# Attention over two pairs of heads at a time: column sums in 32-column quarters of one bank, reciprocals spread by transfers, float32 scores

## The chip, the cores and the metric

The kernel runs on one core of one Trainium2 chip. The metric is the device time of one launch in microseconds (us), a median over runs. The engines are TensorE (PE, with its weight loads as PEld), VectorE (DVE), ScalarE (ACT), GpSimd (POOL) and SyncE (SP), which here only issues transfers.

## What is computed

Float32 throughout, with sizes B=2, H=12, S=448, D=64; 896 tokens of width 768.

```python
scores = cap * tanh(q @ k.T / 8 / cap)            # 24 heads, 448 x 448
attn = exp(scores - max) ; attn /= attn.sum(-1) + 1e-9
x = (attn @ v)                                    # -> 896 x 768
xn = x / sqrt(mean(x*x, -1) + 1e-6) * rms_g
x = (silu(xn @ w_gate) * (xn @ w_val)) @ w_out    # 768 -> 1536 -> 768
out = ((x @ w1) * (x @ w2)) @ w3 @ w_out2         # 768 -> 1024 -> 1024 -> 768
```

## The kernel before

Everything is kept transposed: features on the partitions, tokens on the free axis. The 24 heads form 12 pairs p (a head in rows 0 to 63, the other in rows 64 to 127), and pairs 2d and 2d+1 form a block d of seven groups g (42 groups in all). Keys are cut in chunks of 128, three for each head (c = 0, 1, 2), and 64 keys are left over per head (c = 3). `parts(g)` (L373) says what a group holds: three groups of the even pair, one with the leftovers of both pairs, three of the odd pair. A group passes four steps:

- `scores` (L418, matmul in L430): keys x queries into a double bank `pss` (tag "s", 2 of them), one half for each head. Pair 0 multiplies in float32. For the others `load_head` (L380) splits queries and keys in two fp32r parts (`th`: `half` on ACT or POOL, `rest` L189 on DVE), and three fp32r products are added up. For c < 3 two matmuls with 64 rows each stand in the two row halves of the array; for c = 3 one matmul has 128 rows (the unneeded half of the keys is zero).
- `tanh` (L438) and `exp` (L444) on ACT, into a tile `t` (4 of them).
- `pv` (L448, matmul in L464), once for each pair in the group: the values (64 columns) of both heads into the two column halves of a bank `po`, then 64 columns of ones likewise into a bank `pn`, which gives each column sum 64 times. All four are float32 matmuls; the profile shows each float32 matmul as two records. `po` and `pn` are the two buffers of tag "o", so one pair holds both.
- at a pair's end `take_sum` (L468) and `take` (L478) empty both banks (ACT or DVE), `invert` (L484) takes reciprocals in two pieces (DVE), `normalize` (L491, DVE or POOL) multiplies, `square` (L499, ACT) and `add_square` (L510) gather the squares for the later norm. `normalize_x` (L343) finishes the norm of a batch: `sums` (L305), a root, reciprocals, six products, six splits.

Beside this the first half of the last product, w3 x w_out2, is made from weights alone (`last_product` L609, matmuls L634 to L636): 16 items of four steps of three fp32r matmuls each, into banks of tag "m" (2 of them). It fills PE where nothing else is ready, and most of it comes behind the attention. It reads the tile "B", which the normed x of batch 1 takes over. `weights` (L241) brings every weight tile: a load on SP, two unary operations (ACT or POOL), `join` L270 and `sign` L274 (DVE), a `half` (ACT or POOL) and a `rest` (DVE). `experts` (L719) does the rest of the network in fp32r, its banks taken in turn from tags "m", "o", "s".

The order on every engine is fixed before the launch: `Plan` (L53) holds tasks with a rank, a cost guess for each engine that may do it, and the buffers it makes or uses, and lists them by a simulated clock (`order` L87). Buffers of a tag are handed out in order of the rank of the task that makes them. Each engine then works its list strictly in order.

Of the kernel before, what the change touches and what calls it, by code (L numbers as in the profile page):

```python
# [33 lines left out]
CQ = S // 4  # L34

# [131 lines left out]
def body(ctx: ExitStack, tc, qk, v, cap, wgv, wdn, rg, w12, w3t, wo2, out):  # L167
# [44 lines left out]
    def layer(es, bounded):  # L212
# [5 lines left out]
        rings = dict(qk=2, th=3, v=3, t=4, sm=2, sq=2, s=2, o=2, m=2, raw=NRAW, hl=NHL, mo=2, sg=4, acc=2)  # L218
# [81 lines left out]
        def x_steps(b):  # L300
            st = {}

            def sums(e):
                st["pq"] = bank("o")
                e.matmul(st["pq"][:, :S], ones, acc[b], start=True, stop=True)  # L305
# [37 lines left out]
        def normalize_x(b, after, rank):  # L343
            sums, root, inverse, mul, first, second = x_steps(b)
            pq = buf("o")
# [12 lines left out]
        def attend():  # L358
# [7 lines left out]
            raws, heads, vals, chunks, pos, sums, sqs = {}, {}, {}, {}, {}, {}, {}  # L366
            qkb, thb = {p: buf("qk") for p in range(1, NP)}, {p: buf("th") for p in range(NP)}
            vb, tb, ob = {p: buf("v") for p in range(NP)}, {g: buf("t") for g in range(NG)}, {i: buf("o") for i in range(BH)}
            smb, sqb = {p: buf("sm") for p in range(NP)}, {p: buf("sq") for p in range(NP)}
            first_of = lambda p: 7 * (p // 2) + 3 * (p % 2)  # L370
            h_done, v_done = {}, {}

            def parts(g):  # L373

                d, r = divmod(g, 7)
                if r == 3:
                    return [(2 * d, 3), (2 * d + 1, 3)]
                return [(2 * d + (r > 3), r if r < 3 else r - 4)]

            def load_head(p):  # L380
                def one(e):
                    heads[p] = [ring(ap, "th", [P, 2, S + KP], F32, "qk0")[:, 0]]
                    e.dma_start(out=heads[p][0][:, : S + P], in_=qk[p][:, : S + P])

                def two(e):
                    e.dma_start(out=heads[p][0][:, S + P :], in_=qk[p][:, S + P :])

                def whole(e):
                    raws[p] = ring(ap, "qk", [P, S + KP])
                    e.dma_start(out=raws[p], in_=qk[p])  # L390
# [9 lines left out]
                when = first_of(p) - 7  # L400
                if p == 0:
                    a = add(("SP", 0.45), one, when, makes=[thb[p]], size=P * (S + P) * 4)
                    b = add(("SP", 0.45), two, when + 0.1, behind=[a], uses=[thb[p]], size=P * (KP - P) * 4)
                    h_done[p] = [a, b]
                    return
                a = add(("SP", 0.45), whole, when, makes=[qkb[p]], size=P * (S + KP) * 4)
                r = first_of(p) - 3
                a = add(dict(ACT=1.0, POOL=1.3), first, r, after=[a], makes=[thb[p]], uses=[qkb[p]])
                h_done[p] = [add(("DVE", 1.2), second, r, after=[a], uses=[qkb[p], thb[p]])]
# [38 lines left out]
            def pv(g, j):  # L448

                use = parts(g)  # L450
                p, c = use[j % len(use)]

                def run(e):
                    start = p % 2 == 0 and c == 0 or p % 2 == 1 and c == 3
                    stop = p % 2 == 0 and c == 3 or p % 2 == 1 and c == 2
                    if start:
                        pos[p] = [ring(ps, "o", [P, 512], name=name) for name in ("po", "pn")]
# [10 lines left out]
            def take_sum(pr):  # L468
                def run(e):
                    sums[pr] = ring(ap, "sm", [P, S])  # L470
                    if e is nc.scalar:
                        e.activation(sums[pr], pos[pr][1][:, :S], AF.Identity, bias=guard)
                    else:
                        e.tensor_scalar(sums[pr], pos[pr][1][:, :S], guard, None, op0=ALU.add)  # L474

                return run

            def take(pr):  # L478
                def run(e):
                    half(x_tile(*divmod(pr, H // 2)), pos[pr][0][:, :S], e)  # L480

                return run

            def invert(pr, c):  # L484
                def run(e):
                    r = sums[pr][:, c * S // 2 : (c + 1) * S // 2]
                    e.reciprocal(r, r)  # L487

                return run

            def normalize(pr):  # L491
                def run(e):
                    b, h = divmod(pr, H // 2)
                    x = xraw[b][:, h, :]
                    e.tensor_tensor(x, x, sums[pr], op=ALU.mult)
# [3 lines left out]
            def square(pr):  # L499
                def run(e):  # L500
# [5 lines left out]
                    e.activation(sqs[pr] if h else acc[b], xraw[b][:, h, :], AF.Square)  # L506
# [13 lines left out]
            exps, x_alloc, sq_last, pv_last = {}, {}, {}, {}  # L520
            every = []
            for g in range(NG):
                use = parts(g)
                sb = buf("s")
                qs = [thb[p] for p, _ in use]
# [3 lines left out]
                us = 0.62 * 2 if len(use) == 2 else 0.72  # L529
                if use[0][0] == 0:  # L530
                    us = 0.83 + 0.62 if len(use) == 2 else 0.97
                a = add(("PE", us), scores(g), g - 2, after=need, makes=[sb], uses=qs)
                a = add(("ACT", 1.02), tanh(g), g, after=[a], makes=[tb[g]], uses=[sb])
                exps[g] = a = add(("ACT", 1.06), exp(g), g + 0.1, after=[a], uses=[tb[g]])
                for j in range(len(use)):
                    p, c = use[j]
                    begin = p % 2 == 0 and c == 0 or p % 2 == 1 and c == 3
                    end = p % 2 == 0 and c == 3 or p % 2 == 1 and c == 2
                    both = [ob[2 * p], ob[2 * p + 1]]
                    a = add(  # L540
                        ("PE", 1.65), pv(g, j), g + 1 + 0.1 * j, after=[exps[g], v_done[p], pv_last.get(p)],
                        makes=both if begin else [], uses=[tb[g], vb[p]] + ([] if begin else both),
                    )
# [12 lines left out]
                    every.append(a)  # L556
                    a = add(("ACT", 0.58), square(p), r + 0.4, after=[a], makes=[sqb[p]] if h else [], uses=[xb[b]])
# [51 lines left out]
        def last_product():  # L609
# [16 lines left out]

            def item(kb, n, r):
                def run(e):
                    if r == 0:
                        mb[kb, n] = bank("m")  # L630
# [10 lines left out]
            for kb in range(CF2):  # L641
                bb = [buf("m") for _ in range(2)]
# [13 lines left out]
        def attend_any():  # L656
# [4 lines left out]
            for i in range(BH):  # L661
# [5 lines left out]
                nc.sync.dma_start(out=tv, in_=v[pr])  # L667

# [50 lines left out]
        def experts(over, stored):  # L719
# [258 lines left out]
            for D in range(CD // 2):  # L978
# [72 lines left out]
                for n, (name, op, ready) in enumerate(jobs):  # L1051
# [13 lines left out]
                    tag = ("m", "o", "s")[turn // 2 % 3]  # L1065
# [94 lines left out]
```

## Time and profile before

| | us |
|---|---|
| median of 3 runs (641.0 to 644.27) | 641.41 |
| the profiled execution | 643.46 |
| its span, first to last instruction | 641.7 |
| PE busy | 623.0 (97%) |
| DVE busy | 421.2 (66%) |
| ACT busy | 279.7 (44%) |
| POOL busy | 154.3 (24%) |

The profile lists busy time by engine, then the chain of work that ended last, and groups of instructions by line; the views of the trace cut the same records by stretch, by line, or in order of time. A PE that is busy may be busy with work that another form would need less of; an engine's idle time counts only where PE, or the end, waits for it.

### The profile page before, as it was taken

To read this page: it belongs to the slowest core of one execution; us is meant where nothing else is said; L and a number is where in the kernel's file an instruction comes from. 1 tells how busy PE (TensorE), PEld (TensorE's weight loads), DVE (VectorE), ACT (ScalarE), POOL (GpSimd) and SP (SyncE) were. 2 spreads that over 40 slices of the span, in tenths; PEclk is the share of its full clock that TensorE was granted. 3 is DMA by queue.
4 is the path that set the end of the run, shared out by engine and by line. 5 is a ranking of instruction groups with operands and counts; after the bars stand their busy time and mean duration, and the time that the engine had idled before them with its cause. 6 is when DMAs were issued, how large, how long until landed. Compare 5 with 4: busy or idle time off the path is not lost.

```text
span 641.7 us, 8149 instructions
## 1 busy us (share of the span) xinstructions
PE 623.0 (97%) x3141; PEld 513.8 (80%) x3141; DVE 421.2 (66%) x532; ACT 279.7 (44%) x384; POOL 154.3 (24%) x148
## 2 busy tenths in 40 slices
PE   6989999998999999999999999999999999999995
PEld 2334445468999999999999999999999999999995
DVE  2999969568857778534666555566656765636752
ACT  6878889834634434222334323334423333313230
POOL 2755421002223354321122222211122121100000
PEclk9999999999999999999999999999999999999999
DMA  8445511125634445423994233333232324105111
GB/s 301 127 134 186 166 41 50 34 70 189 227 140 152 148 147 192 153 66 120 314 285 143 99 102 111 129 103 99 98 99 98 110 88 131 34 0 147 54 47 63
DMA packets 29759, 80.18 MB, mean 125 GB/s; under 512 B 2960, under 2 KB 18448, under 8 KB 29712
## 3 DMA queue, kind: packets, MB, share of 16 engines
q1 hardware_dynamic: 29712, 79.58, 37.4%
q8 instruction: 27, 0.44, 0.3%
q14 instruction: 20, 0.16, 0.1%
HBM read 70.52 MB, written 9.04 MB: 124 GB/s over the span
## 4 chain that ended last, share of the span: by engine, by line
PE 89%; DVE 3%; DMA 3%; ACT 2%; POOL 1%; SPq 0%; issue 0%; DVEq 0%; ACTq 0%; POOLq 0%
PE bank L803 22%; PE bank L801 22%; PE bank L802 22%; PE bank L1025 8%; PE po L464 5%; PE pn L464 4%; PE pss L430 4%; DMA wraw<-in_wgv 1%; PE bank L634 1%; DMA wraw<-in_wo 1%; PE bank L636 1%; PE bank L635 1%; DVE sm L487 1%; DVE wraw L274 1%; DVE wraw L270 0%
## 5 line engine op out<-in xcount | busy, mean ns | idle before, releaser
L189 DVE TENSOR_TENSOR whl<-wraw,whl 128x768 fp32r<-128x768 f32 (+1 forms) x86 | 75.9, 884 | 68.3 <-POOL whl L186 55.7
L266 POOL TENSOR_SCALAR wraw<-wraw 128x768 int32<-128x768 uint32 (+1 forms) x67 | 75.1, 1120 | 160.8 <-DMA wraw<-in_w 58.2
L802 PE MATMUL bank<-xn,whl 128*128 128x448 f32 x288 | 105.6, 367 | 0.0
L803 PE MATMUL bank<-xn,whl 128*128 128x448 f32 x288 | 105.6, 367 | 0.0
L801 PE MATMUL bank<-xn,whl 128*128 128x448 f32 x288 | 105.6, 367 | 0.0
L270 DVE SCALAR_TENSOR_TENSOR wraw<-wraw 128x768 int32<-128x768 int32 (+1 forms) x76 | 72.4, 952 | 40.8 <-POOL wraw L266 39.9
L274 DVE SCALAR_TENSOR_TENSOR wraw<-wraw 128x768 int32<-128x768 int32 (+1 forms) x76 | 74.4, 978 | 1.6
L186 POOL TENSOR_SCALAR whl<-wraw 128x768 fp32r<-128x768 f32 (+1 forms) x35 | 32.2, 919 | 171.4 <-PE bank L803 124.1
L182 ACT ACTIVATE whl<-wraw 128x768 fp32r<-128x768 f32 (+1 forms) x51 | 40.7, 800 | 70.9 <-PE bank L803 30.4
L801 PE MATMUL bank<-y,whl 128*128 128x448 f32 x192 | 70.7, 368 | 0.0
L802 PE MATMUL bank<-y,whl 128*128 128x448 f32 x192 | 70.7, 368 | 0.0
L803 PE MATMUL bank<-y,whl 128*128 128x448 f32 x192 | 70.7, 368 | 0.0
L257 ACT ACTIVATE wraw<-wraw 128x768 f32<-128x768 f32 (+1 forms) x57 | 49.8, 874 | 45.5 <-DMA wraw<-in_wgv 15.0
L801 PEld LDWEIGHTS bank<-xn,whl 128*128 128x128 f32 x288 | 54.1, 188 | 4.9
L803 PEld LDWEIGHTS bank<-xn,whl 128*128 128x128 f32 x288 | 54.1, 188 | 4.9
L802 PEld LDWEIGHTS bank<-xn,whl 128*128 128x128 f32 x288 | 54.1, 188 | 4.7
L802 PE MATMUL bank<-u,whl 128*128 128x448 f32 x144 | 52.8, 367 | 0.0
L803 PE MATMUL bank<-u,whl 128*128 128x448 f32 x144 | 52.8, 367 | 0.0
L801 PE MATMUL bank<-u,whl 128*128 128x448 f32 x144 | 52.8, 367 | 0.0
L464 PE MATMUL po<-t,v 128*64 128x448 f32 (+1 forms) x192 | 46.0, 557 | 3.4 <-DVE sm L474 1.8
L438 ACT ACTIVATE t<-pss,small 128x896 f32<-128x896 f32 x42 | 42.0, 999 | 11.9 <-PE pss L430 8.7
L444 ACT ACTIVATE t<-t,small 128x896 f32<-128x896 f32 x42 | 43.8, 1043 | 1.3
(105 smaller groups left out, 1013.5 us busy)
## 6 DMA issues: line engine op xcount, KB each, us to landing
wraw<-in_wgv SPq DMA_DIRECT2D x24, 768.0 KB, 4.6
wraw<-in_w SPq DMA_DIRECT2D x16, 768.0 KB, 4.3
wraw<-in_wdn SPq DMA_DIRECT2D x12, 768.0 KB, 4.3
wraw<-in_w3t SPq DMA_DIRECT2D x16, 512.0 KB, 3.5
wraw<-in_wo SPq DMA_DIRECT2D x8, 768.0 KB, 6.5
qk<-in_qk SPq DMA_DIRECT2D x11, 480.0 KB, 3.7
m_half<-mo SPq DMA_DIRECT2D x16, 192.0 KB, 2.5
mo<-m_half SPq DMA_DIRECT2D x16, 192.0 KB, 5.0
```

The costliest lines, as they stand in the source:

```text
L189: e.tensor_tensor(lo, raw, r32(hi), op=ALU.subtract)
L257: e.activation(h, h, AF.Copy, scale=2.0**-112)
L266: e.tensor_scalar(l, l.bitcast(U32), 0.876 * 2.0**-29, 0.49, op0=ALU.mult, op1=ALU.add)
L270: e.scalar_tensor_tensor(l, h, 3, l, op0=ALU.logical_shift_left, op1=ALU.bitwise_or)
L274: e.scalar_tensor_tensor(l, h, -(2**31), l, op0=ALU.bitwise_and, op1=ALU.bitwise_or)
L438: e.activation(chunks[g], s[:, :, :S], AF.Tanh, scale=tsc)
L444: e.activation(chunks[g], chunks[g], AF.Exp, scale=acap)
L464: e.matmul(pos[p][n][to, :S], w, x, start=start, stop=stop)
L801: e.matmul(dst, whi[:, c, :], src(0, g, b), start=(g == 0), stop=False)
L802: e.matmul(dst, whi[:, c, :], src(1, g, b), start=False, stop=False)
L803: e.matmul(dst, wlo[:, c, :], src(0, g, b), start=False, stop=(g == total - 1))
L1025: e.matmul(st["bank", name], w[:, q, :], z_at(op, q, y), start=q == 0 and n == 0, stop=q == NQ - 1 and n == 2)
```

## The change

Scores are one float32 product for every pair; the splits of queries and keys go. A block's groups alternate between its two pairs, and the leftovers of both come last (r = 6), in four 64 x 64 quarters of the array. `pv` makes values only. The column sums of a block's four heads come from `total`: four matmuls with 32 columns of ones each, which fill the four quarters of one bank (tag "os"), once for each chunk. Sums are emptied and inverted once for each block; `spread` then copies each head's 32 rows of reciprocals to the 64 rows where `normalize` wants them, by four transfers for each pair. Sums are emptied and products taken on DVE only, squares go from ACT to DVE or POOL. "m" has one bank, and the items of the last product behind the fourth take turns between "o", "m" and "s". The layout of the leftover values is swapped for odd pairs.

```diff
-        rings = dict(qk=2, th=3, v=3, t=4, sm=2, sq=2, s=2, o=2, m=2, raw=NRAW, hl=NHL, mo=2, sg=4, acc=2)
+        rings = dict(qk=4, v=4, t=7, sm=2, rb=3, sq=3, s=2, o=2, os=1, m=1, raw=NRAW, hl=NHL, mo=2, sg=4, acc=2)
...
-                st["pq"] = bank("o")
+                st["pq"] = bank("os")
...
+            first_of = lambda p: 7 * (p // 2) + p % 2
...
-                if r == 3:
+                if r == 6:
                     return [(2 * d, 3), (2 * d + 1, 3)]
-                return [(2 * d + (r > 3), r if r < 3 else r - 4)]
+                return [(2 * d + r % 2, r // 2)]
+
+            def across(p, i):
+
+                return slice(D, P) if (p + i) % 2 else slice(0, D)
 
             def load_head(p):
-                def first(e):
-                    t = ring(ap, "th", [P, 2, S + KP], F32R)
-                    heads[p] = [t[:, 0], t[:, 1]]
-                    half(t[:, 0], raws[p], e)
-
-                def second(e):
-                    rest(heads[p][1], raws[p], heads[p][0], e)
-
...
+                when = first_of(p) - (7 if p == 0 else 5)
+                cuts = [slice(0, S + P), slice(S + P, S + KP)] if p == 0 else [slice(0, S + KP)]
...
-                    for n, (x, y) in enumerate(((0, 0), (0, 1), (1, 0))):
-                        for j in range(2):
-                            p, c = use[j % len(use)]
-                            if p == 0 and n:
-                                continue
-                            k, q = heads[p][x], heads[p][y]
-                            rows = slice(j * D, (j + 1) * D) if c < 3 else slice(0, P)
-                            ks = slice(S + c * P, S + (c + 1) * P)
-                            e.matmul(chunks[g][:, j, :S], k[rows, ks], q[rows, :S], start=n == 0, stop=p == 0 or n == 2)
+                    for j in range(2):
+                        for p, c in use:
+
+                            q = heads[p][j * D : (j + 1) * D]
+                            if c < 3:
+                                at, to, ks = j, slice(0, P), slice(S + c * P, S + (c + 1) * P)
+                            else:
+                                at, to, ks = p % 2, across(p, j), slice(S + 3 * P + j * D, S + 3 * P + (j + 1) * D)
+                            e.matmul(chunks[g][to, at, :S], q[:, ks], q[:, :S], start=True, stop=True)
 
                 return run
 
...
-                    for n in range(2):
-                        for i in range(2):
-                            to = slice(i * D, (i + 1) * D)
-                            rows = to if c == 3 else slice(0, P)
-                            x = chunks[g][rows, j if c == 3 else i, :]
-                            w = ones[rows, :D] if n else vals[p][rows, 6 if c == 3 else 2 * c + i, :]
-                            e.matmul(pos[p][n][to, :S], w, x, start=start, stop=stop)
-
...
+            def pv(g):
+
+
+                def run(e):
+                    for i in range(2):
+                        for p, c in parts(g):
+                            if c == 0 and i == 0:
+                                pos[p] = ring(ps, "o", [P, 512], name="po")
+                            rows, n = (slice(0, P), i) if c < 3 else (across(p, i), p % 2)
+                            w = vals[p][rows, 2 * c + i if c < 3 else 6, :]
+                            e.matmul(pos[p][i * D : (i + 1) * D, :S], w, chunks[g][rows, n, :], start=c == 0, stop=c == 3)
+
+                return run
+
+            def total(d, c):
+
+
+                def run(e):
+                    if c == 0:
+                        pns[d] = ring(ps, "os", [P, 512], name="pn")
+                    for q in range(4):
+                        p, i = 2 * d + q // 2, q % 2
+                        g, rows, n = (7 * d + 2 * c + q // 2, slice(0, P), i) if c < 3 else (7 * d + 6, across(p, i), p % 2)
+                        to = slice(q * CW, (q + 1) * CW)
+                        e.matmul(pns[d][to, :S], ones[rows, :CW], chunks[g][rows, n, :], start=c == 0, stop=c == 3)
+
+                return run
+
...
+            def spread(pr, i):
+
+
+                def run(e):
+                    if i == 0:
+                        rbs[pr] = ring(ap, "rb", [P, S])
+                    row = (2 * (pr % 2) + i // 2) * CW
+                    e.dma_start(out=rbs[pr][i * CW : (i + 1) * CW], in_=sums[pr // 2][row : row + CW])
...
-                    e.activation(sqs[pr] if h else acc[b], xraw[b][:, h, :], AF.Square)
+                    x = xraw[b][:, h, :]
+                    e.tensor_tensor(sqs[pr] if h else acc[b], x, x, op=ALU.mult)
...
+                c, last = use[0][1], use[-1][1] == 3
+                a = add(("PE", 0.83), pv(g), g + 1, after=[exps[g]] + [v_done[p] for p, _ in use] + [pv_last.get(p) for p, _ in use],
+                        makes=[ob[p] for p, c in use if c == 0], uses=[tb[g]] + [vb[p] for p, _ in use] + [ob[p] for p, c in use if c])
+                for p, _ in use:
                     pv_last[p] = a
-                    if not end:
-                        continue
-                    b, h = divmod(p, H // 2)
-                    r = g + 1.5
+                if use[-1][0] % 2 == 0:
+                    continue
+                d = g // 7
+                from_ = [g] if last else [g - 1, g]
+                t = add(("PE", 0.83), total(d, c), g + 1.2, after=[exps[x] for x in from_] + [sum_last.get(d)], makes=[] if c else [nb[d]],
+                        uses=[tb[x] for x in from_] + ([nb[d]] if c else []))
+                sum_last[d] = t
+                if not last:
+                    continue
+                r = g + 1.5
+                b = 2 * d // (H // 2)
+                taken = {}
+                got = add(("DVE", 0.64), take_sum(d), r - 2, after=[t], makes=[smb[d]], uses=[nb[d]])
+                for p in (2 * d, 2 * d + 1):
                     new = b not in x_alloc
-                    done = [add(dict(ACT=0.55, DVE=0.64), take_sum(p), r - 2, after=[a], makes=[smb[p]], uses=[both[1]])]
-                    done.append(add(dict(ACT=0.55, DVE=0.64), take(p), r - 1.9, after=[a] + ([] if new else [x_alloc[b]]),
-                                    makes=[xb[b]] if new else [], uses=[both[0]] + ([] if new else [xb[b]])))
-                    x_alloc.setdefault(b, done[1])
-                    inv = [add(("DVE", 1.52), invert(p, c), r + 0.1 * c, after=done, uses=[smb[p]]) for c in range(2)]
-                    a = add(dict(DVE=0.66) if h == 5 else dict(DVE=0.66, POOL=1.3), normalize(p), r + 0.3, after=inv, uses=[smb[p], xb[b]])
+                    taken[p] = add(dict(ACT=0.55, DVE=0.64), take(p), r - 2 + 0.1 * (p % 2), after=[a] + ([] if new else [x_alloc[b]]),
+                                   makes=[xb[b]] if new else [], uses=[ob[p]] + ([] if new else [xb[b]]))
+                    x_alloc.setdefault(b, taken[p])
+                inv = [add(("DVE", 1.52), invert(d, c), r + 0.1 * c, after=[got], uses=[smb[d]]) for c in range(2)]
+                for p in (2 * d, 2 * d + 1):
+                    h = p % (H // 2)
+                    sent = []
+                    for i in range(4):
+                        sent.append(add(("SP", 0.45), spread(p, i), r - 50, after=inv, behind=sent[-1:], makes=[] if i else [rbb[p]], uses=[smb[d]] + ([rbb[p]] if i else []), size=CW * S * 4))
+                    a = add(("DVE", 0.66), normalize(p), r + 0.3, after=sent + [taken[p]], uses=[rbb[p], xb[b]])
                     every.append(a)
-                    a = add(("ACT", 0.58), square(p), r + 0.4, after=[a], makes=[sqb[p]] if h else [], uses=[xb[b]])
+                    a = add(dict(DVE=0.66, POOL=1.3), square(p), r + 0.4, after=[a], makes=[sqb[p]] if h else [], uses=[xb[b]])
...
+            mtag = lambda kb, n: "m" if 2 * kb + n < MB else ("o", "m", "s")[(2 * kb + n - MB) % 3]
...
-                tag = ("m", "o", "s")[turn // 2 % 3]
+                tag = ("m", "o", "s", "os", "o", "s")[turn % 6]
```

## Rows read from the trace of the kernel before

**Rows 1.** The page's busy line of PE: us, share of the span, instructions.
```profile
PE 623.0 (97%) x3141; PEld 513.8 (80%) x3141; DVE 421.2 (66%) x532; ACT 279.7 (44%) x384; POOL 154.3 (24%) x148
```

**Rows 2.** Busy time by stretch: attention, the filler behind it, the experts, the end.
```profile
core 0: us, PE busy (x) PEld busy (x) DVE busy (x) ACT busy (x) POOL busy (x), PEclk, DMA share, GB/s
5.10:135.75 130.65, 126.52 (x677) 55.96 (x677) 105.05 (x109) 105.60 (x122) 50.57 (x44) 1.00 0.37 123
135.75:165.03 29.28, 26.59 (x151) 25.92 (x150) 22.52 (x25) 13.36 (x21) 5.39 (x7) 1.00 0.56 184
165.03:634.94 469.91, 469.87 (x2317) 431.88 (x2316) 292.06 (x391) 159.30 (x240) 97.93 (x92) 1.00 0.37 123
634.94:641.70 6.76, 0.00 (x0) 0.00 (x0) 0.62 (x1) 0.00 (x0) 0.00 (x0) 0.84 0.13 42
```

**Rows 3.** Waits of PE over the span: us in total, times, longest.
```profile
PE pss L430 <- DMA qk<-in_qk: 5.1, 1, 5.1
PE bank L634 <- ACT mo L182: 2.7, 1, 2.7
PE po L464 <- DVE sm L474: 1.8, 2, 1.3
PE po L464 <- DVE xraw L184: 1.5, 1, 1.5
PE pss L430 <- ACT t L438: 0.6, 2, 0.4
```

**Rows 4.** Busy time by stretch of L464 alone: PE, PEld, then clock and DMA.
```profile
5.10:135.75 130.65, 79.58 (x384) 24.22 (x384) 1.00 0.37 123
```

**Rows 5.** The chain of work, 44 to 64 us: start, us, what.
```profile
46.54 0.90 PE po L464 x4
47.44 0.75 PE pn L464 x4
...
49.70 0.80 PE pss L430 x6
```

**Rows 6.** PE in order of time around a leftover group: start, us.
```profile
39.06 0.97 PE L464 MATMUL po<-t,v 64*64 64x448 f32 x4
39.87 0.92 PE L464 MATMUL pn<-t,ones 64*64 64x448 f32 x4
40.72 0.87 PE L430 MATMUL pss<-th 64*128 64x448 f32 x6
```

**Rows 7.** Groups by line and form, 0 to 170 us: busy us, mean ns | idle before.
```profile
L444 ACT ACTIVATE t<-t,small 128x896 f32<-128x896 f32 x42 | 43.8, 1043 | 1.3
L438 ACT ACTIVATE t<-pss,small 128x896 f32<-128x896 f32 x42 | 42.0, 999 | 11.9 <-PE pss L430 8.7 <-PE pn L464 2.9
L487 DVE RECIPROCAL sm<-sm 128x224 f32<-128x224 f32 x24 | 35.6, 1522 | 1.0 <-ACT sm L472 0.8
L189 DVE TENSOR_TENSOR th<-qk,th 128x960 fp32r<-128x960 f32 x11 | 13.7, 1249 | 5.1 <-ACT th L182 5.1
L464 PEld LDWEIGHTS pn<-t,ones 128*64 128x64 f32 x144 | 10.3, 137 | 16.7 <-issue 16.7
L506 ACT ACTIVATE sq<-xraw 128x448 f32<-128x448 f32 x10 | 5.8, 576 | 7.5 <-POOL xraw L495 4.1 <-DVE xraw L495 3.2
L513 DVE TENSOR_TENSOR acc<-acc,sq 128x448 f32<-128x448 f32 x8 | 5.4, 676 | 1.4 <-ACT sq L506 1.4
```

**Rows 8.** Pair 0's three float32 score groups: by form, and the third in time.
```profile
L430 PE MATMUL pss<-qk 64*128 64x448 f32 x12 | 4.0, 820 | 5.1 <-DMA qk<-in_qk 5.1
...
8.16 0.93 PE L430 MATMUL pss<-qk 64*128 64x448 f32 x4
```

**Rows 9.** Loads at the start: one stretch (columns as rows 2), the page's issue line.
```profile
6.00:7.00 1.00, 1.00 (x6) 0.59 (x4) 0.00 (x0) 0.00 (x0) 0.00 (x0) 1.00 0.92 312
...
qk<-in_qk SPq DMA_DIRECT2D x11, 480.0 KB, 3.7
```

**Rows 10.** Tile mo to 170 us: the landing of its 192 KB transfers.
```profile
DMA to landing us min/median/max: 1.8/2.5/8.1
```

**Rows 11.** The chain of work behind the attention: start, us, what.
```profile
142.54 8.43 DMA wraw<-in_wgv
```

More of the change, by code (lines that the diff above doesn't have):

```diff
@@ L34 @@
 CQ = S // 4
+CW = P // 4
+MB = 4
 BOUND = 40.0
@@ L365, in attend @@
             NP = BH // 2
[L366 to L370, printed above, removed]
+            heads, vals, chunks, pos, pns, sums, rbs, sqs = {}, {}, {}, {}, {}, {}, {}, {}
+            qkb = {p: buf("qk") for p in range(NP)}
+            vb, tb, ob, nb = {p: buf("v") for p in range(NP)}, {g: buf("t") for g in range(NG)}, {p: buf("o") for p in range(NP)}, {d: buf("os") for d in range(NP // 2)}
+            smb, sqb = {d: buf("sm") for d in range(NP // 2)}, {p: buf("sq") for p in range(NP)}
+            rbb = {p: buf("rb") for p in range(NP)}
+            first_of = lambda p: 7 * (p // 2) + p % 2
             h_done, v_done = {}, {}
@@ L385, in two @@
[L385 to L390, printed above, removed]
-                def first(e):
-                    t = ring(ap, "th", [P, 2, S + KP], F32R)
-                    heads[p] = [t[:, 0], t[:, 1]]
-                    half(t[:, 0], raws[p], e)
-                def second(e):
-                    rest(heads[p][1], raws[p], heads[p][0], e)
@@ L400, in load_head @@
[L400 to L408, printed above, removed]
@@ L409, in load_head, with run @@
-                h_done[p] = [add(("DVE", 1.2), second, r, after=[a], uses=[qkb[p], thb[p]])]
+                def run(e, cols, new):
+                    if new:
+                        heads[p] = ring(ap, "qk", [P, S + KP])
+                    e.dma_start(out=heads[p][:, cols], in_=qk[p][:, cols])
+                when = first_of(p) - (7 if p == 0 else 5)
+                cuts = [slice(0, S + P), slice(S + P, S + KP)] if p == 0 else [slice(0, S + KP)]
+                h_done[p] = []
+                for n, c in enumerate(cuts):
+                    h_done[p].append(
+                        add(("SP", 0.45), lambda e, c=c, n=n: run(e, c, n == 0), when + 0.1 * n, behind=h_done[p], makes=[] if n else [qkb[p]], uses=[qkb[p]] if n else [],
+                            size=P * (c.stop - c.start) * 4)
+                    )
@@ L471, in run, with take_sum @@
+            def take_sum(d):
+                def run(e):
+                    sums[d] = ring(ap, "sm", [P, S])
                     if e is nc.scalar:
-                        e.activation(sums[pr], pos[pr][1][:, :S], AF.Identity, bias=guard)
+                        e.activation(sums[d], pns[d][:, :S], AF.Identity, bias=guard)
                     else:
-                        e.tensor_scalar(sums[pr], pos[pr][1][:, :S], guard, None, op0=ALU.add)
+                        e.tensor_scalar(sums[d], pns[d][:, :S], guard, None, op0=ALU.add)
@@ L479, in run, with invert @@
                 def run(e):
-                    half(x_tile(*divmod(pr, H // 2)), pos[pr][0][:, :S], e)
+                    half(x_tile(*divmod(pr, H // 2)), pos[pr][:, :S], e)
                 return run
-            def invert(pr, c):
+            def invert(d, c):
                 def run(e):
-                    r = sums[pr][:, c * S // 2 : (c + 1) * S // 2]
+                    r = sums[d][:, c * S // 2 : (c + 1) * S // 2]
                     e.reciprocal(r, r)
+                return run
[5 more added lines that the diff above has]
+                    e.dma_start(out=rbs[pr][i * CW : (i + 1) * CW], in_=sums[pr // 2][row : row + CW])
                 return run
@@ L494, in run @@
                     x = xraw[b][:, h, :]
-                    e.tensor_tensor(x, x, sums[pr], op=ALU.mult)
+                    e.tensor_tensor(x, x, rbs[pr], op=ALU.mult)
                 return run
@@ L519, in attend @@
                 load_val(p)
-            exps, x_alloc, sq_last, pv_last = {}, {}, {}, {}
+            exps, x_alloc, sq_last, pv_last, sum_last = {}, {}, {}, {}, {}
             every = []
@@ L524, in attend @@
                 sb = buf("s")
-                qs = [thb[p] for p, _ in use]
+                qs = [qkb[p] for p, _ in use]
                 need = []
@@ L528, in attend @@
                     need += h_done[p][:1] if p == 0 and c == 0 else h_done[p]
[L529 to L532, printed above, removed]
+                a = add(("PE", 0.83), scores(g), g - 2, after=need, makes=[sb], uses=qs)
                 a = add(("ACT", 1.02), tanh(g), g, after=[a], makes=[tb[g]], uses=[sb])
@@ L629, in run @@
                     if r == 0:
-                        mb[kb, n] = bank("m")
+                        mb[kb, n] = bank(mtag(kb, n))
                     whi, wlo = w3[kb]
@@ L641, in last_product @@
             for kb in range(CF2):
-                bb = [buf("m") for _ in range(2)]
+                bb = [buf(mtag(kb, n)) for n in range(2)]
                 last = {}
@@ L667, in attend_any @@
                 nc.sync.dma_start(out=tv, in_=v[pr])
+                if pr % 2:
+                    for j in range(2):
+                        nc.sync.dma_start(out=tv[j * D : (j + 1) * D, 6], in_=v[pr][(1 - j) * D : (2 - j) * D, 6])
                 off = one * (KP - S)
@@ L1125, in _layout @@
     v = a["v"].reshape(BH // 2, 2, S, D)
-    both = np.concatenate([v[:, 0, 3 * P :], v[:, 1, :D]], axis=1)[:, None]
+    both = np.stack([v[:, 0, 3 * P :], v[:, 1, :D]], axis=1)
+    both[1::2] = both[1::2, ::-1].copy()
+    both = both.reshape(-1, 1, P, D)
     v = np.stack([v[:, 0, : 3 * P].reshape(-1, 3, P, D), v[:, 1, D:].reshape(-1, 3, P, D)], axis=2).reshape(-1, 6, P, D)
```

25 lines of the change are left out of this document (2 added, 23 removed).

## The prediction

> **What bounds the kernel now.** I read the busy line first: PE is busy for 623.0 us of 641.7 [rows 1], so 18.7 us are idle, and any gain must come from less PE work or from that rest. Busy time by stretch comes next [rows 2]: the experts, 165.03 to 634.94, have PE busy for 469.87 of 469.91 us. The change leaves that stretch's products as they are, so its length stays and the question is only when it starts. The waits of PE [rows 3] place the idle time: 5.1 for the first load, 3.9 in the attention (1.8 and 1.5 for DVE emptying the banks of a pair, 0.6 for ACT), 2.7 behind it, and 6.76 at the end when the last output leaves [rows 2]. In the attention DVE is busy for 105.05 us and ACT for 105.60 of 130.65 [rows 2]: loaded, but PE seldom waits for either. So this is a PE sum, with DVE, ACT and transfers as possible new limits.
>
> **PE, values and sums.** Line 464 costs 79.58 us [rows 4] for 48 calls of `pv` (12 pairs, four chunks), 1.66 each: 0.90 for the values and 0.75 for the ones that follow [rows 5]. 0.75 is two float32 matmuls side by side in two column halves; the 0.15 above it falls on the first step after one of another tile shape. After the change there are 42 `pv` and 24 `total` (six blocks, four chunks), each a step of another shape than the one before it: 42 x 0.90 + 24 x 0.90 = 59.4. That is 20.2 less.
>
> The open price is that of four tiles at once, which no row shows. The lower bound is 0.75, as for two tiles [rows 5], or less than nothing extra where two steps of one shape meet (0.15 saved each). The upper bound is 1.50, two at a time, at each of 24 `total`, six leftover scores and six leftover `pv`. One reason for a small surplus: a 64-column weight load takes 137 ns [rows 7], and four of them in a row, 0.55, exceed the 0.375 of one of the two passes; that would make a `total` 1.10, 24 x 0.35 = 8.4 us more. But these loads run beside matmuls (24.22 us of them under 79.58 of matmuls [rows 4]) and 32 columns should need less. I take 0.75 plus the 0.15, nearest to the rows that show two tiles without any loss.
>
> The Trainium skill, TensorE: Matmul & The Clock Gate, section "Measured speedup vs the span model", has three column tiles at 2.38 times one, not 3. An estimate by it, a surplus of a quarter on each `total`, would add 24 x 0.19 = 4.6 us to my sum; no run here shows three or four tiles.
>
> **PE, scores.** A fp32r group costs 0.80 behind a `pv` [rows 5]. What is left of the stretch's 126.52 busy us, without the 79.58 of line 464 and some 10 of filler and norm (16 triples at 0.52, one 0.75, and shape changes), is 37 for 42 groups, 0.88 each (the leftover groups are dearer). A float32 group is two passes of two row halves: 0.75 + 0.15 = 0.90, 42 x 0.90 = 37.8, so 1 us more. Pair 0 speaks against it at first sight: its three float32 groups took 4.0 us, 1.33 each, with records of 820 ns [rows 8]. But that includes waiting, and the third, all four of its records, took 0.93 with its drain [rows 8], as a `po` step does in the same kind of view (0.97 [rows 6]). Were it 1.33 everywhere, 42 x 0.43 = 18 us would be added; a rival. PE in all: 20.2 - 1.0 = 19.2 less.
>
> **The start.** Group 1 now belongs to pair 1, so its scores wait for 480 KB more [rows 9], where before three groups of pair 0 ran on the first load. Behind the first 288 KB, which land at 5.1, stand 192, twice 224 and 480 KB, 1.15 MB; at 312 GB/s [rows 9] that is 3.7 us, 8.8 in all, and later if the weight loads behind share. Group 0 ends at about 6.5 (its records are slow [rows 8]), so PE loses about 2.5 us (bounds 0, if ACT sets the pace there anyway, to 5).
>
> **What leaves DVE, ACT and POOL.** The eleven splits of queries and keys take 13.7 us of DVE, half of 24 reciprocals 17.8 [rows 7]; squares come to DVE or POOL, at most 12 x 0.676 = 8.1 by the row of the nearest product [rows 7], and five products come from POOL to DVE, 3.4. DVE has about 20 us less, 85 for a stage of some 113. All this is off PE's path and worth only the waits of rows 3: 3.3 of the 3.9 are DVE's. I count 1.5 of them, since the new `po` banks are both in use and a block's end still waits for both to be emptied. ACT loses 12 squares (6.9) and about 4.5 of splits and sums. The splits that leave ACT and POOL free them for weight steps; I count nothing.
>
> **What is added off PE.** 48 spread transfers of 57 KB wait on SP for the reciprocals; queued behind them on SP are loads of later heads and weights, which are asked for five groups (some 11 us) ahead, so nothing is counted. Each `normalize` on DVE waits for its four transfers, with weight steps and the next squares queued behind it. The nearest row, 192 KB, lands in 1.8 to 8.1, median 2.5 [rows 10]; I take 2.5 with the issues before it, hidden under DVE's 28 us of slack. At the end of the attention the chain to the norm of batch 1 gains a spread and a second pair, perhaps 5 us; it is covered by the remaining items (at least nine of 2.1 us, 19) and by the four early products on batch 0. The cover before was 29.28 [rows 2]; if it fails, up to 5 us show. The stall of 2.7, a bank emptied late because ACT stood waiting for a load of 8.43 us [rows 3, 11], is kept (0 to 6).
>
> With one "m" bank an item waits for the emptying of the one before; attention work stands between, so nothing is counted, and moving items behind the attention moves PE work without adding any.
>
> **The sum.** Span: 641.70 - 19.2 + 2.5 - 1.5 = 623.5. The profiled execution adds 1.76 (643.46 - 641.70): 625.3. It is 2.05 above the median, so on the scale of the median **623.2 us**, 2.8% less.
>
> **Rivals.**
> 1. *ACT sets the pace of the attention.* Tanh and exp take 2.04 a group [rows 7]; the other ACT work of the stage, 105.6 - 85.8 - 11.4 = 8.4, adds 0.20. That is 2.24 against PE's 97.2 / 42 = 2.31, where before it stood at 2.51 against 2.78. For it: the margin shrinks from 0.27 to 0.07, and only two score banks stand between the engines. Against: `t` grows from 4 to 7 and items fill PE's gaps. Waits of 0.15 a group give 42 x 0.15 = 6: 629.5. Chance 0.18.
> 2. *DVE waits for the spreads.* DVE's slack of 28 us over 12 pairs is 2.3 each; it decides from a landing of 2.5 + 2.3 = 4.8 us behind the weight loads in the queues. At 6 us PE would lose 12 x 1.2 = 14: 637. For it: the 8.1 of rows 10. Against: half the landings are at 2.5 or less. Chance 0.10.
> 3. *Four tiles run two at a time,* slower than before: 36 steps x 0.75 = 27, 650. It decides from 0.5 us a step, where the gain is gone. For it: nothing shows four. Against: two halves of the array work with no loss in both directions, and four quarters are the same thing twice. Chance 0.08; float32 scores at 1.33 (641) have 0.02 more.
> 4. *Two row halves can't write one bank at once,* which the leftover scores and the leftover `total` do: 12 x 0.75 = 9, 632. The rows speak against it: in the leftover `pv` of before both row halves write one bank, and it takes 0.81 and 0.85 from start to start [rows 6], no more than the rest. The Trainium skill, TensorEngine Tiling (Array Packing), section "Gotcha 1: PSUM Pressure", says that different row tiles cannot access the same bank simultaneously; by that rule this rival holds, and the trace disagrees for halves of the partitions. Chance 0.02.
>
> That the change doesn't do what it says would be rival 3: sums of 32 columns that cost what 64 did.
>
> **How the numbers follow.** The forecast, PE's sum, has 0.60 and a range of its own of 614 to 630 (below: waits of 3.9 and 2.7 gone and shapes that meet, 9; above: weight loads not hidden and a late norm). A measurement of this kernel can tell about 0.5% from no change. Faster, under 638.2: 0.60 + 0.18 + 0.06 of rival 2 + 0.02 = 0.86. Slower, over 644.6: 0.08 + 0.02 = 0.10. Within: 0.04. The range that should hold 8 in 10 is 614 to 636; it takes in rival 1, rival 4 and the early part of rival 2.
>
> **What would show it.** In the profile after: line 464's values and the `total` steps at 0.75 to 0.90 from start to start, together near 59 us; L430 near 38; PE's busy time near 604; the first experts' product at about 147 instead of 165, and from there the same 470 us; a wait of PE for pair 1's load near 2.5. `total` near 1.65 would show rival 3; PE waiting for `t` over 42 groups rival 1; DVE idle ahead of `normalize` by more than 28 us in all rival 2. The prediction is wrong if the experts' stretch itself changes length, or if PE's idle time grows by more than 8 us.

## The result, and the profile after

The changed kernel takes 624.96 us (624.79 to 625.47) against 641.87 (641.0 to 644.27): a ratio of 0.9732, 95% interval 0.9704 to 0.976. The forecast was 623.2. The profiled execution took 625.47 with a span of 623.3; the sum had 625.3 and 623.5.

The page's busy line of the changed kernel, and what PE waited for (us in total, times, longest), as [rows 1] and [rows 3] of before:

```profile
PE 608.6 (98%) x3088; PEld 490.6 (79%) x3088; DVE 401.0 (64%) x527; ACT 265.7 (43%) x359; POOL 141.6 (23%) x138
...
PE pss L421 <- DMA qk<-in_qk: 5.1, 1, 5.1
PE po L449 <- ACT t L435: 2.2, 1, 2.2
PE bank L826 <- DVE whl L191: 0.8, 2, 0.6
PE bank L654 <- DVE mo L186: 0.4, 1, 0.4
PE bank L824 <- ACT mo L184: 0.3, 1, 0.3
```

PE's busy time fell by 14.4 us, not by 19.2, and its idle time fell from 18.7 to 14.7, where the sum had let it grow by 1.0. The waits for DVE in the attention are gone, all of them. Busy time by stretch (columns as [rows 2]: start, attention, hand-over to the experts):

```profile
5.10:15.00 9.90, 7.66 (x22) 2.39 (x24) 2.46 (x3) 4.26 (x5) 4.12 (x4) 1.00 1.02 401
15.00:114.50 99.50, 99.50 (x580) 26.56 (x580) 75.60 (x93) 86.83 (x93) 30.39 (x29) 1.00 0.42 135
114.50:160.00 45.50, 44.03 (x239) 41.36 (x236) 37.65 (x46) 21.08 (x34) 11.35 (x11) 1.00 0.60 192
```

From 15 us to the last sums at 114.5 PE is never idle; before, the attention ran to 135.75 [rows 2]. The chain of work of the changed kernel shows what a step costs from start to start (L449 values, L463 sums, L421 scores; the last two lines are leftovers of a block):

```profile
100.61 0.90 PE po L449 x4
101.52 0.89 PE pn L463 x8
102.41 0.95 PE pss L421 x4
106.83 0.91 PE pss L421 x8
...
113.68 0.93 PE pn L463 x8
```

Four tiles of 32 columns (0.89), and four quarters of 64 x 64 (0.91), cost what two tiles cost before (0.90 [rows 5]), each with its change of shape. The first products of the experts start at 145.68 instead of 165.03 (147 was said).

### The profile page after: what moved, and what is told of

Same layout as the page of the kernel before. It is cut to its first block, busy times and chain, and to the rows that moved or that the text cites. A ratio compares the mean times of both kernels' runs of the same rounds, so it can differ in the third digit from the quotient of the medians.

```text
span 623.3 us, 8065 instructions
## 1 busy us (share of the span) xinstructions
PE 608.6 (98%) x3088; PEld 490.6 (79%) x3088; DVE 401.0 (64%) x527; ACT 265.7 (43%) x359; POOL 141.6 (23%) x138
## 4 chain that ended last, share of the span: by engine, by line
PE 91%; DMA 3%; DVE 2%; ACT 2%; issue 1%; SPq 0%; DVEq 0%; ACTq 0%
PE bank L826 22%; PE bank L825 22%; PE bank L824 22%; PE bank L1048 8%; PE pss L421 6%; PE po L449 6%; PE pn L463 3%; DMA wraw<-in_wgv 2%; DMA m_half<-mo 1%; DMA qk<-in_qk 1%; DVE whl L191 1%; DVE xraw L322 0%; ACT xn L184 0%; DVE sm L486 0%; ACT t L435 0%
## 5 line engine op out<-in xcount | busy, mean ns | idle before, releaser
L191 DVE TENSOR_TENSOR whl<-wraw,whl 128x768 fp32r<-128x768 f32 (+1 forms) x86 | 74.5, 867 | 69.5 <-POOL whl L188 58.5
L259 ACT ACTIVATE wraw<-wraw 128x768 f32<-128x768 f32 (+1 forms) x54 | 47.5, 882 | 45.4 <-DMA wraw<-in_wgv 17.3
L421 PE MATMUL pss<-qk 64*128 64x448 f32 (+1 forms) x192 | 44.5, 604 | 5.1 <-DMA qk<-in_qk 5.1
```

The costliest lines, as they stand in the source:

```text
L191: e.tensor_tensor(lo, raw, r32(hi), op=ALU.subtract)
L259: e.activation(h, h, AF.Copy, scale=2.0**-112)
L421: e.matmul(chunks[g][to, at, :S], q[:, ks], q[:, :S], start=True, stop=True)
```

## Experiments

The expectations were written after the result was known. All times are medians, with the ratio to the kernel before on the same chip and its interval.

**1. The sums made twice** (the sums come out doubled; the order of work is kept).

```diff
-                    for q in range(4):
+                    for k in range(8):
+                        q = k % 4
...
-  ... start=c == 0, stop=c == 3)
+  ... start=c == 0 and k < 4, stop=c == 3 and k > 3)
```

> The changed kernel with each of the 24 steps of column sums made twice into the same bank (so the sums come out doubled; x is halved and the norm behind it takes the factor out). The planner's costs and so the order of all work stay as they were; only PE gets more. The theory (PE's work sets the time, and four 32-column tiles run at once) expects 24 x 0.75 = 18 us more: 643, within 2. If ACT set the pace of the attention, PE would have room and less than 10 us would show: under 635. If four tiles ran two at a time, a step would cost 1.5 more and 36 us would show: 661.

Measured: 644.10, ratio 1.001 (0.9988 to 1.0031). Against the changed kernel's 0.9732 that is 2.9%, 17.9 us. The page's busy line:

```profile
PE 627.0 (98%) x3280; PEld 497.1 (77%) x3280; DVE 399.5 (62%) x527; ACT 265.9 (41%) x359; POOL 143.6 (22%) x138
```

PE's busy time grew by 18.4 and the time by 17.9: work put on PE in the attention counts in full, and four tiles of 32 columns run at once. Rivals 1 and 3 of the prediction fall.

**2. The reciprocals made twice, in the order of the changed kernel.**

```diff
+                    e.reciprocal(scratch, r)
                     e.reciprocal(r, r)
```

> The changed kernel with each of its 12 reciprocals of the sums made once more into a scratch tile ahead of the true one, in the same order of work: 12 x 1.52 = 18.2 us of DVE put back, as many reciprocals as in the kernel before, and 3 us more between a block's last sums and its spread. The theory (DVE's relief lies off PE's path) expects no more than 1.5 us: 625 to 626.5. The rival, that a part of the gain is DVE's relief (the waits of 3.3 us for emptied banks and of 2.7 us behind the attention are gone in the changed kernel), expects 3 to 6 us: 628 to 631.

Measured: 634.94, ratio 0.9884 (0.9858 to 0.991): 10 us more than the changed kernel. The theory as it stood fell, and by more than the rival had said. PE's waits:

```profile
PE po L450 <- ACT t L436: 4.8, 3, 2.2
PE bank L307 <- DVE acc L526: 2.8, 1, 2.8
PE pn L464 <- DVE sm L474: 1.7, 1, 1.7
```

New are 1.7 for the bank of sums, 2.8 for the squares of a batch, and 2.6 more for ACT. From 15 to 100 us PE is busy for 79.21 of 85 us, where the changed kernel has all 85. But this kernel has two faults at once: more DVE work, and an order that doesn't know of it. The next runs take them apart.

**3. The same with the cost told to the planner** (3.04 instead of 1.52).

> As the kernel with the reciprocals made twice, but with their cost told to the planner (3.04 us a piece instead of 1.52), so that the order of all work is made with it. If DVE's load itself stands close to PE's path, 18.2 us of it cost here too: 631 to 637. If the earlier loss came from engines that stood in a fixed order waiting for a late DVE, most of it goes: 625 to 628.

Measured: 632.98, ratio 0.9858 (0.9836 to 0.988), 8 us more. The first answer, DVE's load, seemed right; the trace placed the loss elsewhere. Of this run, two stretches and the one large new wait of PE:

```profile
15.00:100.00 85.00, 84.83 (x490) 22.01 (x490) 75.14 (x86) 76.71 (x84) 30.68 (x30) 1.00 0.45 151
...
147.00:160.00 13.00, 8.40 (x29) 7.12 (x30) 10.61 (x16) 8.77 (x14) 1.10 (x1) 0.74 0.62 214
...
PE bank L826 <- ACT mo L184: 4.1, 1, 4.1
```

With DVE at 75.14 of 85 us PE still loses nothing in the attention. It waits 4.1 at the hand-over, and then its products run slow: 29 in 13 us, with the wait, at a granted clock of 0.74, where the 15 us behind that hold 76 at full clock.

**4 and 5. The last block's reciprocals twice; the first five blocks' twice** (both planned).

```diff
+                    if d == NP // 2 - 1:        # d < NP // 2 - 1 in the other
+                        e.reciprocal(scratch, r)
```

> The changed kernel with the reciprocals of the last block alone made twice (into a scratch tile first), the planner told: 3.0 us more DVE work, all of it in the chain between the last sums and the norm of batch 1. Theory after the planned repeat of all of them (+8 us, with PE's waits all behind the attention): what counts is the chain behind the attention, so the last block alone brings most of it: 629 to 633. Rival: it is the sum of DVE's work over the attention, of which this is a sixth: 625 to 627.

> The counterpart: the first five blocks' reciprocals twice, the last block's once, the planner told: 15.2 us more DVE work, none of it in the last chain. Theory (the chain behind the attention): 625 to 627. Rival (the sum of DVE's work): five sixths of the 8 us, 631 to 632.

Measured: 629.47, ratio 0.9806 (0.9786 to 0.9825), for 3 us more in the last block; 625.38, ratio 0.9735 (0.9717 to 0.9753), for 15.2 us more in the first five. So DVE work in the attention costs nothing that can be measured if the order is made for it, and 3 us behind it cost 4.5. The first row below is of the run with the first five blocks: DVE is busy for 73.74 of 85 us. Up to 114.5 us its DVE is busy for 87.14 us against 79.00 in the changed kernel, so 8.1 of the 15.2 are more work there; the new order has less other work of DVE in that time. The other rows are of the run with the last block: ACT in order of time, then PE.

```profile
15.00:100.00 85.00, 84.83 (x490) 21.99 (x490) 73.74 (x85) 75.99 (x84) 29.98 (x29) 1.00 0.45 152
...
146.70 2.93 ACT L184 ACTIVATE xn<-xraw 128x448 fp32r<-128x448 f32 x6
149.50 0.88 ACT L184 ACTIVATE mo<-bank 128x384 f32<-128x384 f32 x2
...
150.06 0.47 PE L827 MATMUL bank<-xn,whl 128*128 128x448 f32 x1 [4.21 <-ACT mo L184]
...
151.23 0.58 PE L828 MATMUL bank<-xn,whl 128*128 128x448 f32 x1
151.60 0.58 PE L829 MATMUL bank<-xn,whl 128*128 128x448 f32 x1
```

The changed kernel in the same place, ACT in order of time, then PE:

```profile
146.48 0.48 ACT L184 ACTIVATE mo<-bank 128x384 f32<-128x384 f32 x1
146.85 2.91 ACT L184 ACTIVATE xn<-xraw 128x448 fp32r<-128x448 f32 x6
149.66 0.48 ACT L184 ACTIVATE mo<-bank 128x384 f32<-128x384 f32 x1
...
145.68 0.36 PE L824 MATMUL bank<-xn,whl 128*128 128x448 f32 x1
...
150.19 0.47 PE L824 MATMUL bank<-xn,whl 128*128 128x448 f32 x1 [0.27 <-ACT mo L184]
```

In both kernels PE's last item ends at about 145.7. Then the six first halves of the normed x go through ACT, since the tile "B" is free at last. Behind them, at about 149.6 in both, ACT empties a bank that PE needs. In the changed kernel PE starts the experts at 145.68 in a bank that is free already; the second chain of products, 18 products later, needs the late bank and waits 0.27. In the other kernel the first product needs it, PE waits 4.21, and its products then come 0.37 apart instead of 0.20. Worked out from the two kernels' fixed lists, the first chain stands in a bank of tag "o" in the changed kernel and in the one bank of tag "m" in the other; the emptying of "m" stands behind the six in both. The 4.5 us are thus an order on PE, which a chain 3 us longer had brought about, and the slow products behind the gap. The lists of runs 3, 6 and 8 have "m" first too, and each waits 3.5 to 4.1 there; the runs whose lists have "o" first (1, 2, 5, 9, 10 and 11) wait 0.4 for it at most. Whether the 3 us would cost anything in the old order wasn't tried.

**6. Squares on ACT, as before.**

```diff
-                    e.tensor_tensor(sqs[pr] if h else acc[b], x, x, op=ALU.mult)
+                    e.activation(sqs[pr] if h else acc[b], x, AF.Square)
```

> The changed kernel with the squares on ACT as before, which takes 6.8 us from DVE and gives 6.9 to ACT over the attention, and 1.2 us from DVE in the chain behind it. If only that chain counts: no change or up to 1.5 us less, 623.5 to 625.5. If ACT sets the pace of the attention (86.3 of 98.6 us busy there): 628 or more.

Measured: 633.32, ratio 0.9868 (0.9848 to 0.9887), 8.4 more. Both expectations fail in their reason. PE waits for `t` no more than in the changed kernel, so ACT does not set the pace. The loss is again the hand-over:

```profile
PE bank L824 <- ACT mo L184: 3.5, 1, 3.5
PE po L449 <- ACT t L435: 2.2, 1, 2.2
...
122.86 0.96 PE L463 MATMUL pn<-t,ones 64*32 64x448 f32 x8
```

Here PE did more items inside the attention, the last sums came at 122.86 instead of 113.61, and fewer items were left to cover the chain to the norm of batch 1. But PE waits for a bank here and not for that norm. The first product of the experts starts at 150.94, 5.3 us later than in the changed kernel: 3.5 are the wait, as in run 4, and 1.8 lie ahead of it in PE's own work. The products behind the wait are slow as well (0.77 of the clock in 145 to 160 us). The profiled execution was the fastest of the four, 6.1 us above that of the changed kernel; the rest of the 8.4 has no trace.

**7. Float32 scores alone, in the kernel before.**

```diff
-                k, q = heads[p][x], heads[p][y]     # three products of split parts
+                k, q = heads[p][0], heads[p][0]     # one float32 product; no splits
```

> The kernel before with float32 scores alone: no splits of queries and keys, all else as before. The theory (PE's work sets the time) expects it slower than the kernel before: 33 groups at 0.95 instead of 0.80, and leftover groups of two full float32 steps, 1.65 instead of 1.42: 5.0 + 1.3 = 6 us, less up to 3.3 of waits for DVE: 645 to 648. The rival (DVE's relief of 13.7 us and ACT's and POOL's of 11.7 are worth something) expects no change or faster: 642 or less.

Measured: 643.04, ratio 1.001 (0.9987 to 1.0032): no change; the expected 645 to 648 are missed. PE's busy time rose to 629.6, by 6.6, as expected. But PE's waits are down to this:

```profile
PE pss L419 <- DMA th<-in_qk: 5.1, 1, 5.1
PE po L453 <- DVE sm L463: 1.4, 2, 1.2
```

Of the 6.6 us of waits behind the first load [rows 3] 1.4 are left. So this part of the change costs PE 6.6 of work and gives 5.2 back in waits; PE's idle time as a whole fell by 6.2, from 18.7 to 12.5. Of the waits for DVE alone, 3.3 before, 1.4 stay.

**8 and 9. The changed kernel with the scores of before, and its base with small rings alone.**

```diff
-        rings = dict(qk=4, v=4, t=7, sm=2, rb=3, sq=3, ...
+        rings = dict(qk=4, v=4, t=4, sm=2, rb=2, sq=2, ...            # base
+        rings = dict(qk=2, th=3, v=4, t=4, sm=2, rb=2, sq=2, ...      # with load_head and splits of before
```

> The changed kernel with the scores of before (fp32r in three products from split queries and keys; leftovers with 128 rows), in smaller rings to make room (4 tiles t, 2 of reciprocals, 2 of squares). PE's work alone: 33 groups at 0.80 instead of 0.95, six leftover groups at 1.42 instead of 0.91: 2 us less than the changed kernel, 623. If DVE's load stands close to the path, its 13.7 us of splits (and 11.7 on ACT and POOL) cost more than that: 628 to 632.

> The changed kernel with the smaller rings of the kernel with fp32r scores and nothing else: 4 tiles t instead of 7, 2 of reciprocals and 2 of squares instead of 3. It is the base for that kernel. The theory expects no change, 624 to 626.5; if the larger rings carry a part of the gain, 628 or more.

Measured: 637.91, ratio 0.9914 (0.9883 to 0.9946), and the base 625.50, ratio 0.974 (0.9716 to 0.9764). The larger rings carry nothing that can be measured. The splits put back cost 12.4 us, more than expected. PE's waits with them:

```profile
PE pss L439 <- DVE th L191: 3.6, 3, 1.5
PE bank L842 <- ACT mo L184: 3.5, 1, 3.5
PE po L467 <- ACT t L453: 2.4, 2, 2.2
PE bank L307 <- DVE acc L542: 1.4, 1, 1.4
```

3.6 are PE waiting for the splits themselves, 1.4 for squares, 3.5 the hand-over again. The two profiled runs lie 12.7 us apart. Of these 6.0 stand ahead of the hand-over's wait: the first product of the experts starts at 155.81 behind a wait of 3.47, in the base at 146.37 behind none. The rest is that wait, slow products behind it, and 0.6 at the end, and belongs to the order as in run 4. So float32 scores pay in the changed kernel, though they cost PE more: without them, in the order that the planner made, the shortened sums bring only 0.9%.

**10. Without the spread** (the product takes the reciprocals of other heads).

```diff
-                    e.dma_start(out=rbs[pr][i * CW : (i + 1) * CW], in_=sums[pr // 2][row : row + CW])
+                    rbs[pr] = sums[pr // 2]
```

> The changed kernel without the 48 spread transfers; the product takes the tile of sums as it stands, that is, the reciprocals of other heads (the spread is left out, so x is not right). The order of all other work stays. The theory (the transfers are hidden) expects 624 to 625.5, no change against the changed kernel. The rival, that DVE's 9.2 us of waiting ahead of the product hold weights or banks back, expects 3 us or more: 622 or less.

Measured: 622.93, ratio 0.9689 (0.9664 to 0.9714), in neither of the expected ranges. By the ratios that is 2.8 us below the changed kernel, and the intervals overlap (0.9704 to 0.976 there), so whether the transfers cost something stays open. In the trace of this run, its slowest execution, the first product of the experts starts at 145.72, as in the changed kernel. In the changed kernel's trace they land in 1.9 to 3.2 us, median 2.0, and DVE waits 9.2 us for them in five places.

**11. Work for PE ahead of the first scores.**

```diff
+                    if g == 0:
+                        spare = bank("m")
+                        for _ in range(9):        # 8 more behind the scores of group 0
+                            e.matmul(spare[:, :P], ones, ones, start=True, stop=True)
```

> The changed kernel with nine products of the tile of ones ahead of the first scores and eight behind them, into a bank that nobody reads, all in time in which PE waits. The order of the rest stays. In the changed kernel the passes of the first 10 us take twice as long as later (1.76 instead of 0.90 for the first values, three score groups in 4.06 instead of 2.86), and three of these steps stand in the chain of work. Theory: it is PE's earlier idleness that does it, and work ahead takes it away: 2.0 to 2.8 us less, 622 to 623. Rival: the first steps are slow for another reason (the loads' traffic, say), and nothing changes: 624.5 to 625.5.

The start in the changed kernel and in this one, PE in order of time:

```profile
5.10 1.86 PE L421 MATMUL pss<-qk 64*128 64x448 f32 x4 [5.10 <-DMA qk<-in_qk]
9.15 1.76 PE L449 MATMUL po<-t,v 128*64 128x448 f32 x4 [2.18 <-ACT t L435]
10.84 4.00 PE L421 MATMUL pss<-qk 64*128 64x448 f32 x12
```

```profile
0.99 4.03 PE L414 MATMUL bank<-ones 128*128 128x128 f32 x18 [0.99 <-POOL ones L201]
5.02 1.02 PE L425 MATMUL pss<-qk 64*128 64x448 f32 x4
5.97 2.05 PE L428 MATMUL bank<-ones 128*128 128x128 f32 x16
8.22 0.97 PE L456 MATMUL po<-t,v 128*64 128x448 f32 x4 [0.20 <-ACT t L442]
```

Measured: 624.30 (623.21 to 625.55), ratio 0.9724 (0.9702 to 0.9745). The slow steps are gone (0.95 instead of 1.89 for the first scores, 0.91 instead of 1.7 for the first values), and the profiled run is 2.3 us shorter than that of the changed kernel; but the median is only 0.7 less, within the intervals. The granted clock fits: the record of it in the trace begins, at full, at 13.4 us in the changed kernel, at 8.1 in the kernel before and at 4.7 here, each time where the slow steps end. The 1.00 of the column ahead of that stands for the lack of a record. That PE's idleness ahead makes these steps slow is settled, the gain is not.

**12. A faster version: the same, with the spread of the last pair on ACT.**

```diff
-                        sent.append(add(("SP", 0.45), spread(p, i), ...
+                        sent.append(add(("ACT" if p == NP - 1 else "SP", 0.45), spread(p, i), ...
```

> The kernel with the products of ones at the start, and the spread of the last pair issued on ACT instead of SP, so that the last block's eight transfers go out in two queues: the second pair's four land about 2.4 us earlier. Theory (the chain behind the attention counts, and the start): 1.5 to 2.5 us less than with the products of ones alone, 622 to 623. Rival (both are covered by the remaining items): 624 to 625.

Measured: 621.43 (621.36 to 622.36), ratio 0.9676 (0.9661 to 0.969), 3.5 us below the changed kernel and clear of its interval. PE's waits behind the first scores add up to 1.3 us:

```profile
PE bank L831 <- ACT mo L184: 0.7, 1, 0.7
PE pss L425 <- ACT t L436: 0.4, 1, 0.4
PE po L456 <- ACT t L442: 0.2, 1, 0.2
```

It beats both kernels. It is 2.9 us below run 11, which has the first of its two edits, with intervals apart (0.969 and 0.9702); the second edit alone wasn't run. Its order is another one too: the first product of the experts needs the bank "m" here, but that emptying stands ahead of the six halves, and PE waits 0.7. So how much the earlier transfers themselves give is not shown.

## Why the prediction was right, point by point

The total was right to 0.3%, and the direction for the reason given: PE's work. But PE's work and PE's idle time were each mis-sized by nearly 5 us, in opposite directions, and cancelled: that the total is so close is luck.

- *Values and sums.* Right: 42 x 0.90 + 24 x 0.89 = 59.2 against 59.4. The open price, four tiles at once, was 0.89 with the change of shape, no more than two tiles. An estimate by the Trainium skill, TensorE: Matmul & The Clock Gate, "Measured speedup vs the span model" (2.38 for three column tiles), would have put 4.6 us on top; the trace disagrees for these float32 steps (0.89).
- *Two row halves in one bank.* The leftover scores take 0.91 and the leftover sums 0.93 with the drain, so rival 4 is out. The rule of the Trainium skill, TensorEngine Tiling (Array Packing), "Gotcha 1: PSUM Pressure", that different row tiles cannot access one bank at once, does not hold here for halves that write different partitions.
- *Scores.* Mis-sized: 0.95 a step and not 0.90, since the change to this shape costs 0.20 and not 0.15; 36 x 0.95 + 6 x 0.91 = 39.7 instead of 37.8, 1.9 more.
- *The start.* The size was right (2.2 idle, 2.5 said), the reason wrong. PE did not wait for pair 1's load: the planner had put the first values ahead of group 1's scores, and PE waited for `exp`. And a cost was missed: PE ran at half pace from its first product until 13.4 us (8.1 in the kernel before), 0.9 more for the first scores, 0.86 for the first values and 1.2 for three score groups, 3.0 in all. The 1.33 of pair 0's groups [rows 8], explained away as waiting, was this. With the scores that is 4.9, and the experts' stretch holds 0.8 more of busy time (470.6 against 469.9); PE's busy time missed 4.8, so these shares are good to about 1 us.
- *Waits for DVE.* Mis-sized the other way: 1.5 of the waits were to go, and 3.9 in the attention and 1.2 of 2.7 at the hand-over went; the end behind PE's last product is 0.9 shorter too. In the kernel before, float32 scores alone take 5.2 of the 6.6 us of waits away (run 7), but of DVE's 3.3 only 1.9; what took the others wasn't tried by itself. That DVE's load in the attention has room is shown by the five blocks (0.4 us for 15.2).
- *Rivals.* ACT's pace (0.18): no wait for `t` between 15 and 114.5 us with ACT at 86.83 of 99.5. Spreads: landings of 2.0 in the median, 3.2 at most, under the 4.8 from which it was to decide. Two tiles at a time: excluded by run 1 and by the trace.
- *The chain behind the attention* was called covered, with up to 5 us if not. It is covered in the changed kernel. But three edits that changed the order there (runs 3, 4 and 6) cost 4.5 to 8.4, by a bank that comes late and not by the norm itself.
- *The experts' stretch* was to keep its length, or the prediction would be wrong. It grew a little, from 469.9 to 471.7, with 1.1 of waits that now fall into it.

## What to carry to other kernels

Where an engine is busy for 97% of the span, sum its work by start-to-start times from the chain, and put a price of its own on every change of tile shape. Waits of a few us for other engines belong to the sum as well: a change that takes work off those engines can give back what its dearer form costs. At the hand-over between two stages, look at which bank the first product takes and what stands ahead of its emptying: giving the first product the bank that six other instructions kept waiting cost 4.2 us there, and 15 us of planned DVE work inside the stage cost nothing that could be measured.

## What the runs showed of the hardware

- Four float32 tiles of 128 x 32 or 64 x 64 run at once, at 0.89 and 0.91 us for 448 columns with the change of shape, as two of 128 x 64 do (0.90).
- Behind the wait of 4.21 us in run 4 PE's products come at half pace, 0.37 apart instead of 0.20, at the lower of the two levels of its clock (1.2 against 2.4 GHz); the granted clock shows it (0.74 in 147 to 160 us of run 3). At the start, behind 5.1 us without work and a wait of 2.18, the steps take twice as long as later (1.7 instead of 0.91 for the first values) until the record of the granted clock begins, at full. Products of no use in the gaps took these slow steps away (run 11).
- A transfer of 57 KB from one tile to another lands in 2.0 us in the median (1.9 to 3.2, 48 of them).
